# Another order for the opening of an FNet mixing and GeGLU kernel, with the −2·O weights made on GpSimd

## Chip, core and metric

The kernel runs on one core of a Trainium2 chip. The metric is the device time of one execution in microseconds (us). Its engines are called here TensorE (PE in the profile; PEld is its weight load), VectorE (DVE), ScalarE (ACT), GpSimd (POOL) and SyncE (SP, which only issues transfers here).

## What is computed

```python
def _attn_ref(x):                      # x: 8 x 3008 x 256, float32
    X = np.fft.fft(x, axis=1)
    X = np.fft.fft(X, axis=2)
    return X.real.astype(np.float32)

def _moe_ref(x, w_gate, w_val, w_out): # 24064 x 256, 256 x 1536 twice, 1536 x 256
    g = x @ w_gate
    gelu = 0.5 * g * (1.0 + erf(g * np.float32(1.0 / np.sqrt(2.0))))
    val = x @ w_val
    return (gelu * val @ w_out).astype(np.float32)
```

The second is applied to the rows of the first.

## The kernel before, in words

**The mixing.** The DFT over the 3008 tokens is split as 64 times 47. A batch entry is loaded twice, forward and mirrored (a row-indexed transfer on POOL, L163). Folds (`fold_ops`, L221, L222, L225, and for later entries L229) add and subtract the two into `eo`, in five pieces of positions: (13,4), (9,4), (5,4), (1,4) and (0,1), written as (first position, how many). Matmuls with a table `G` follow (`s1`, L508, in four groups of two halves for the first entry; `s1t`, L549, for the others), then for the first entry a combination through identity matrices (`ch`, L530) into `Z`, then matmuls with a table `TP` (`tp_e`, L585 and L590) into two halves `E` and `O`, and a helper row `EB` (`tp_y`, L609). The DFT over the 256 channels is folded into the gate and value weights: `make_w` (L448) multiplies the raw weights by a table `CW`, and its results are evacuated from PSUM into `W_sb` by ACT (L454) or DVE (L456). All tables are computed in the kernel: phases on DVE (`reduced`, L265, L266), sines on ACT (L351 to L374, L408).

**The feed-forward part.** A row t of the spectrum and the row T−t share `E` and `O`: one is E+O and the other E−O. For each of the 12 slices of 128 hidden columns, a gate matmul on E and one on O (L668) give the first row's gate, ACT takes its GELU (L684), and a third matmul with the weights −2·O (called `M`; `l1_gate2`) turns the same PSUM bank into the mirrored row's gate, for a second GELU (L693). In the first chunk's slices 0 to 7 the value does the same with an `M` of its own (`three`, `V3_TO` = 1024 columns; L707 and L724 are the products on DVE). In all other slices the mirrored value is made on DVE (L712, L730) and the product on POOL (L732). L757 multiplies the products by the output weights `Wo_sb`.

**What sets the order.** Every engine executes in the order in which the code emits (`manual_schedule`). `opening()` emits the tables, loads, folds and matmuls of the first entry. `feed()` then emits numbered steps, one for each slice of each chunk (12 steps a chunk, 3 chunks an entry). Step i emits, in this order: gate E and O of slice i; gate M of slice i−1; value of slice i; POOL work from `plan()`; value M or O of slice i−1; and the `fill` of that step from `plan()`. The fills of steps 0 to 7 are the remaining `make_w`: columns 256 to 511 in step 0, 512 to 1023 in steps 1 to 3, 1024 to 1535 in steps 4 to 7. From step 4 on `plan()` gives POOL the folds of the second entry.

**POOL's queue in the opening.** POOL issues 21 transfers in this order: numbers 1 to 5 bring the first entry's rows that are not in `x_stage` (SP brings that one); 6 to 13 are the raw weights, gate and value by turns in column ranges of 256, 256, 512 and 512 (L428); 14 to 19 bring the second entry (L185, L163); 20 and 21 are the two halves of the output weights (`load_wo`, L434). The raw weights and the entries 1 to 5 and 14 to 19 are converted to bf16 on the way.

**The M weights.** `make_w` with part 1 makes O; `minus()` inside it makes M by scaling the PSUM bank with a column `keep2` (−2, and 0 in row 0), on ACT (L463) or on DVE (L465). For columns 0 to 255 the call is held back to the end of the opening.

**Filler matmuls.** `warm(n)` (L828) issues n matmuls of zeros, whose result nobody reads.

Of the kernel before, what the change touches and what calls it, by code (L numbers as in the profile page):

```python
# [10 lines left out]
BF16 = mybir.dt.bfloat16  # L11
AF = mybir.ActivationFunctionType
ALU = mybir.AluOpType
# [15 lines left out]
def kernel(  # L29
# [212 lines left out]
    row_j = const_pool.tile([128, NJ], FP32)  # L242
    row_k = const_pool.tile([128, NK], FP32)
    row_c = const_pool.tile([128, 128], FP32, name="row_c")
    par = const_pool.tile([1, 5, 128], FP32)
    one = const_pool.tile([1, 2], FP32)
    parc = const_pool.tile([128, 5], FP32)
# [16 lines left out]
    def reduced(d, r, f):  # L264
        nc.vector.tensor_scalar(r, f, MAGIC, None, op0=ALU.add)  # L265
        nc.vector.scalar_tensor_tensor(d, r, MAGIC, f, op0=ALU.subtract, op1=ALU.subtract)  # L266
# [14 lines left out]
    def pool_consts2():  # L281
        nc.gpsimd.iota(row_c, pattern=[[1, 128]], base=0, channel_multiplier=0, **IOTA)
        nc.gpsimd.iota(par[:, 0, :], pattern=[[1, 16], [0, 8]], base=1, channel_multiplier=0, **IOTA)
        nc.gpsimd.iota(row_t, pattern=[[1, K1]], base=0, channel_multiplier=0, **IOTA)

    def par_n1():

# [76 lines left out]

    def cw_phases():
        nc.scalar.activation(cf[:, 0:128], row_c, AF.Copy, scale=col_n0)
        reduced(cd[:, 0:128], cr[:, 0:128], cf[:, 0:128])

    def cw_magnitude():
        nc.scalar.activation(cf[:, 128:256], cd[:, 0:128], AF.Abs)  # L370
# [5 lines left out]
    def cw_rest():  # L376


        nc.vector.tensor_copy(CW[:, 0, 0, 0:1], col_e)
        nc.vector.tensor_copy(CW[:, 1, 0, 0:1], col_h)  # L380
        for i, sign in enumerate((1.0, -1.0)):
            nc.vector.tensor_scalar(
                _sub(CW, [[256, 2], [2, 64]], 128 + i), _sub(CW, [[256, 2], [2, 64]], i), sign, None, op0=ALU.mult)
        nc.vector.tensor_copy(CW[:, 1, 1, 0:1], col_h)

    def identities():
# [2 lines left out]
            _sub(II, [[128, 3], [1, 128]], 0), _sub(row_c, [[0, 3], [1, 128]], 0), col_p, None, op0=ALU.is_equal)  # L389
        nc.vector.tensor_scalar(II[:, 1, 1, :], row_c, col_p, -1.0, op0=ALU.is_equal, op1=ALU.mult)  # L390

    def t_columns():
        ps = psum("v")
        for i in range(5):
            nc.tensor.matmul(ps[:, i : i + 1], par[:, i, :], one[:, int(i == 0) : int(i == 0) + 1], start=True, stop=True)
        nc.scalar.activation(parc, ps[:, 0:5], AF.Copy)

    def t_phases():
        k1 = _sub(row_t, [[1, K1]], 0)
        for i in range(2):  # L400
            nc.scalar.activation(
                tf[:, i * K1 : (i + 1) * K1], k1, AF.Identity, scale=parc[:, 0:1], bias=parc[:, 1 + i : 2 + i])

    def t_reduced():
        reduced(td[:, :], tr[:, :], tf[:, :])
# [33 lines left out]

    V3_TO = 1024  # L440

    def make_w(i, f0, n, parts=(0, 1), engine="A", m_at=None, tag="dft"):

        def run():
            ps = psum(tag)
            for k, part in enumerate(parts):
                for half in range(2):
                    nc.tensor.matmul(  # L448
                        ps[:, k * n : (k + 1) * n], CW[:, part, half, :], w_raw[:, i, half, f0 : f0 + n],
                        start=half == 0, stop=half == 1)  # L450
            m = n * len(parts)
            dst = _sub(W_sb, [[F, len(parts)], [1, n]], (2 * i + parts[0]) * F + f0)
            if engine == "A":
                nc.scalar.activation(dst, ps[:, :m], AF.Copy)  # L454
            else:
                nc.vector.tensor_copy(dst, ps[:, :m])  # L456
            if 1 in parts and (i == 0 or f0 < V3_TO):
                def minus():
                    if i and f0 == 0:
                        W["v", "M"] = work([128, V3_TO], BF16, "osb", 3, "w_minus")[:, :]  # L460
                    dst, src = W["gv"[i], "M"][:, f0 : f0 + n], ps[:, m - n : m]
                    if engine == "A":
                        nc.scalar.activation(dst, src, AF.Copy, scale=keep2)  # L463
                    else:
                        nc.vector.tensor_scalar(dst, src, keep2, None, op0=ALU.mult)  # L465

                if m_at is None:
                    minus()
                else:
                    m_at.append(minus)  # L470
        return run
# [44 lines left out]
                nc.vector.tensor_copy(dst, src)  # L516
        return run

    def ch(b, pp, engine="A"):

        def run():
            st = state(b)
            A = st["A"]
            if "Z" not in st:
                st["Z"] = Z_tile()
            ps = ps_any(b)
            for q in range(2):
                k = 2 * (2 * pp + q)
                for g in range(2):
                    nc.tensor.matmul(  # L530
                        ps[:, q * C : (q + 1) * C], _sub(A, [[1, 128]], g * NK * K1 + k * K1), II[:, g, :, :],
                        start=g == 0, stop=g == 1)
            dst = _sub(st["Z"], [[1, 512]], pp * 512)
            if engine == "A":
                nc.scalar.activation(dst, ps[:, :], AF.Copy)
            else:
                nc.vector.tensor_copy(dst, ps[:, :])
        return run

    def s1t(b, jg, half):  # L540
# [252 lines left out]
    def opening():  # L793
        stage[0] = stage_tile()
        xb[0] = xb_tile(0)
        for j0, nj, at in ((9, 8, 0), (0, 1, 8)):
            nc.sync.dma_start(
                out=_sub(stage[0], [[1, nj * C]], at * C),
                in_=ap_replace(x, ap=[[32 * C, NPX], [1, nj * C]], offset=x.offset + j0 * C))
        pool_consts()  # L800
        index_consts(0)
        cast_mirror(0, 9, 8)
        pool_consts2()
        cast_mirror(0, 5, 4)
        cast_forward(0, 1, 8)
        index_consts(1)
        cast_mirror(0, 0, 1)
        cast_mirror(0, 1, 4)
        for f0, n in ((0, 256), (256, 256), (512, 512), (1024, 512)):
            load_w(f0, n)  # L810
        xb[1] = xb_tile(1)
        cast_forward(1, 9, 8)
        cast_mirror(1, 9, 8)
        cast_forward(1, 0, 9)
        for j0, nj in ((5, 4), (1, 4), (0, 1)):
            cast_mirror(1, j0, nj)
        for q in range(2):
            load_wo(q)
        idle = gelu_tile()[:, 0, :]
        nc.vector.memset(one[:, 0:1], 1.0)  # L820
        sin_table()
        nc.vector.memset(idle, 0.0)

        def warm(n):

            ps = psum("o")
            for _ in range(n):
                nc.tensor.matmul(ps[:, :], idle[:, 0:128], idle[:, :], start=True, stop=True)  # L828

        def fold_piece(j0, nj):  # L830
            for f in fold_ops(0, j0, nj, nc.vector):
                f()

        vec_consts()
        vec_fills()
        warm(7)
        g_phases()
        t_columns()
        t_phases()
        g_rows(9, 7)  # L840
        t_reduced()
        vec_consts2()
        identities()
        cw_phases()
        g_ends()
        cw_magnitude()
        vec_fills2()
        g_rows(1, 8)
        t_sin()
        cw_sin()  # L850
        gelu_table()
        warm(6)
        fold_piece(9, 4)
        s1(0, 2, 0)()
        s1(0, 2, 1)()
        warm(8)
        fold_piece(13, 4)
        cw_rest()
        fold_piece(5, 4)
        s1(0, 1, 0)()  # L860
        s1(0, 1, 1)()
        warm(2)
        fold_piece(0, 1)
        s1(0, 3, 0)()
        s1(0, 3, 1)()
        fold_piece(1, 4)
        t_write()
        s1(0, 0, 0)()
        s1(0, 0, 1, "V")()
        minus = []  # L870
        make_w(0, 0, 256, m_at=minus, tag="o")()
        ch(0, 0)()
        ch(0, 1, "V")()
        make_w(1, 0, 256, m_at=minus, tag="g")()
        tp_e(0, 0, 0, "V", tag="v")()
        tp_e(0, 0, 1, "A", tag="v")()
        minus[0]()
        minus[1]()

    def behind_first_gate():  # L880
        tp_y(0, 0)()

    NS = NG * NFC

    def plan():
# [8 lines left out]
            e = "A" if gi == 1 else "V"  # L894
            early += [ch(0, 2 * gi), ch(0, 2 * gi + 1, e), tp_e(0, gi), tp_o(0, gi, e), tp_y(0, gi)]
        for s, f in (
                (0, make_w(0, 256, 256)), (0, make_w(1, 256, 256, engine="V")), 
                (1, make_w(1, 512, 512, (1,))), (2, make_w(0, 512, 512, (0,), "V")), 
                (3, make_w(0, 512, 512, (1,))), (3, make_w(1, 512, 512, (0,), "V")),
                (4, make_w(1, 1024, 512, (1,), "V")), (5, make_w(0, 1024, 512, (0,), "V")),   # L900
                (6, make_w(0, 1024, 512, (1,))), (6, make_yw()), (7, make_w(1, 1024, 512, (0,), "V"))):
            at(fill, s, f)
        for i, f in enumerate(early):
# [56 lines left out]
    def feed():  # L960
# [11 lines left out]
        for i, (parts, fc) in enumerate(blocks):  # L972
# [2 lines left out]
                pend = list(works[i // NFC - 1])  # L975
            two = sooner.pop(i, []) if i <= NFC + 2 else [pend.pop(0) for _ in range(2) if pend]
            parts["G"][fc]()
            if i == 0:
                behind_first_gate()
            if before:  # L980
                before[0]["g"][before[1]]()
            parts["V"][fc]()
# [49 lines left out]
```

## Time and profile before

| what | us |
|---|---|
| median of 8 runs (622.64 to 624.59) | 623.57 |
| the profiled execution's own time | 623.46 |
| its span, first to last instruction | 621.4 |
| TensorE busy | 609.8 (98%) |
| VectorE busy | 576.7 (93%) |
| GpSimd busy | 504.5 (81%) |
| ScalarE busy | 426.3 (69%) |
| first matmul of the feed-forward part starts at | 19.00 |

The profile is of one execution. Times in it count from the span's start; the execution's own time is 2.06 us longer than the span. A row of its timeline has a start, a length, the engine, the source line, the operation, output <- input, and how many instructions were merged; in brackets stands the engine's idle time before the row and what ended it. A row of its stages has the stretch of time, then each engine's busy time (with the number of instructions), the granted TensorE clock (1.00 is full speed), the share of the 16 DMA engines that was busy, and GB/s.

### The profile page before, as it was taken

The page shows a single profiled execution, that of the slowest core. Times are in us where ns is not written, and L with a number is a line of the kernel's source. Part 1 is how long each engine was busy: PE and PEld are TensorE (multiplying, and loading weights), DVE is VectorE, ACT ScalarE, POOL GpSimd, SP SyncE. Part 2 cuts the span into 40 slices and gives each one's busy share as a digit, 9 for nine tenths or more (in the row PEclk, how much of TensorE's full clock was granted, in tenths as well). Part 3 has the DMA queues.
Part 4 walks back from the last instruction along what each step waited for, and adds up shares of the span by engine and source line. Part 5 has one row for each costly group of instructions (what it writes and reads, how often), then busy time and mean ns, then how long its engine had stood idle before and what let it go on. Part 6 is the DMA issues. An engine that isn't in the chain of part 4 may idle for free.

```text
span 621.4 us, 12788 instructions
## 1 busy us (share of the span) xinstructions
PE 609.8 (98%) x4229; PEld 405.7 (65%) x4229; DVE 576.7 (93%) x939; ACT 426.3 (69%) x827; POOL 504.5 (81%) x510
## 2 busy tenths in 40 slices
PE   7999999999999999999999999999999999999997
PEld 3456666666666666666666666666666666666666
DVE  8688998999999999999999999999999999999992
ACT  6877667767776677667766677767676667666661
POOL 8399899999997999879997899969987555555651
PEclk8999999999999999999999999999999999999999
DMA  9961736555463353631644335543122321221123
GB/s 180 232 94 27 202 99 155 119 138 150 114 152 94 103 139 90 177 107 43 168 122 120 103 87 133 136 108 93 48 65 70 95 68 47 65 52 41 42 52 82
DMA packets 52464, 65.40 MB, mean 105 GB/s; under 512 B 7627, under 2 KB 47276, under 8 KB 50002
## 3 DMA queue, kind: packets, MB, share of 16 engines
q1 hardware_dynamic: 45470, 49.03, 30.4%
q0 software_dynamic: 6608, 15.29, 11.6%
q8 instruction: 33, 0.54, 0.4%
q10 hardware_dynamic: 320, 0.26, 0.2%
q14 instruction: 33, 0.27, 0.2%
HBM read 39.65 MB, written 30.17 MB: 112 GB/s over the span
## 4 chain that ended last, share of the span: by engine, by line
PE 90%; POOL 4%; issue 2%; DVE 2%; ACT 1%; DMA 1%; SPq 0%; ACTq 0%; POOLq 0%; DVEq 0%
PE ps_o L757 37%; PE ps_g L668 28%; PE ps_v L668 19%; PE ps_dft L549 2%; POOL h_sb L732 2%; PE ps_dft L585 1%; PE ps_o L828 1%; DMA out_dram<-out_sb 1%; POOL eo_sb L229 1%; POOL ab_sb L222 1%; PE ps_dft L448 0%; POOL ab_sb L225 0%; ACT gelu_sb L693 0%; DVE h_sb L724 0%; ACT gelu_sb L684 0%
## 5 line engine op out<-in xcount | busy, mean ns | idle before, releaser
L732 POOL TENSOR_TENSOR h_sb<-gelu_sb,v_sb 128x512 bf16<-128x512 bf16 (+1 forms) x280 | 319.4, 1145 | 88.4 <-DVE v_sb L730 83.0
L757 PE MATMUL ps_o<-Wo_sb,h_sb 128*128 128x256 bf16 (+1 forms) x2232 | 334.7, 273 | 0.8 <-POOL h_sb L732 0.8
L757 PEld LDWEIGHTS <-h_sb 128*128 128x128 bf16 (+1 forms) x2304 | 228.7, 100 | 112.2 <-POOL h_sb L732 2.4
L684 ACT ACTIVATE gelu_sb<-ps_g 128x512 bf16<-128x512 f32 (+1 forms) x288 | 169.6, 589 | 99.8 <-PE ps_g L668 90.0
L712 DVE SCALAR_TENSOR_TENSOR ve_sb<-EB_sb,yw,ps_v 128x512 f32<-128x512 bf16 (+1 forms) x280 | 206.3, 737 | 22.8 <-PE ps_v L668 18.8
L668 PEld LDWEIGHTS <-W_sb 128*128 128x128 bf16 x1440 | 138.0, 98 | 81.5 <-issue 4.1
L728 DVE TENSOR_TENSOR h_sb<-gelu_sb,ps_v 128x512 bf16<-128x512 bf16 (+1 forms) x280 | 189.7, 677 | 1.1 <-ACT gelu_sb L693 0.7
L730 DVE SCALAR_TENSOR_TENSOR v_sb<-ve_sb,ps_v 128x512 f32<-128x512 f32 (+1 forms) x280 | 187.3, 669 | 0.0
L668 PE MATMUL ps_g<-O_sb,W_sb 128*128 128x512 bf16 (+1 forms) x576 | 168.9, 374 | 0.4 <-DMA O_sb<-yrow 0.3
L693 ACT ACTIVATE gelu_sb<-ps_g 128x512 bf16<-128x512 f32 (+1 forms) x288 | 169.1, 587 | 0.0
L668 PE MATMUL ps_g<-E_sb,W_sb 128*128 128x512 bf16 (+1 forms) x288 | 108.0, 375 | 0.8 <-ACT gelu_sb L693 0.5
L668 PE MATMUL ps_v<-E_sb,W_sb 128*128 128x512 bf16 (+1 forms) x288 | 108.0, 375 | 0.6 <-DVE W_sb L456 0.4
L668 PE MATMUL ps_v<-O_sb,W_sb 128*128 128x512 bf16 (+1 forms) x288 | 108.0, 375 | 0.0
L777 ACT ACTIVATE out_sb<-ps_o 128x512 f32<-128x512 f32 x92 | 54.9, 597 | 35.3 <-PE ps_o L757 35.1
L229 POOL TENSOR_TENSOR eo_sb<-ab_sb 94x512 bf16<-94x512 f32 (+1 forms) x70 | 77.7, 1112 | 0.4
L552 ACT ACTIVATE S_sb<-ps_dft 96x512 bf16<-96x512 f32 x56 | 33.0, 589 | 18.8 <-PE ps_dft L549 18.8
L225 POOL TENSOR_TENSOR ab_sb<-x_raw,x_raw 94x508 f32<-94x508 f32 (+1 forms) x30 | 33.0, 1099 | 0.0
L222 POOL TENSOR_TENSOR ab_sb<-x_raw,x_raw 94x508 f32<-94x508 f32 (+1 forms) x30 | 33.0, 1099 | 0.0
L549 PE MATMUL ps_dft<-eo_sb,G 94*96 94x256 bf16 x119 | 22.3, 272 | 0.5 <-POOL eo_sb L229 0.5
L595 ACT ACTIVATE E_sb<-ps_dft 128x512 bf16<-128x512 f32 (+1 forms) x23 | 13.5, 588 | 8.7 <-PE ps_dft L585 8.7
L163 POOL DMA_INDIRECT x_raw<-in_x_dram,idx x18 | 17.0, 946 | 2.9 <-issue 1.4
L595 ACT ACTIVATE O_sb<-ps_dft 128x512 bf16<-128x512 f32 (+1 forms) x22 | 12.9, 589 | 7.3 <-PE ps_dft L585 6.7
(151 smaller groups left out, 203.7 us busy)
## 6 DMA issues: line engine op xcount, KB each, us to landing
out_dram<-out_sb SPq DMA_DIRECT2D x364, 64.0 KB
x_raw<-in_x_dram SPq DMA_DIRECT2D x10, 768.0 KB
Z_sb<-z SPq DMA_DIRECT2D x7, 768.0 KB
z<-S_sb SPq DMA_DIRECT2D x7, 576.0 KB
EB_sb<-yrow SPq DMA_DIRECT2D x6, 376.2 KB
z<-S_sb SPq DMA_DIRECT2D x7, 192.0 KB
x_raw<-in_x_dram SPq DMA_DIRECT2D x2, 640.0 KB
x_stage<-in_x_dram SPq DMA_DIRECT2D x1, 768.0 KB
```

Source lines behind the costliest of these rows:

```text
L222: eng.tensor_tensor(ab(0, 1, up), fwd(1, up), mir(255, down), op=ALU.add)
L229: eng.tensor_tensor(_sub(eo, [[C, nj], [1, 128]], j0 * C + g * 128), ab(0, 0, [[1, 128]]), ab(1, 0, [[1, 128]]), op=op)
L549: nc.tensor.matmul(ps[:96, q * C : (q + 1) * C], G[:, j, :], _sub(eo, [[1, C]], j * C), start=(j == js[0]), stop=(j == js[-1]))
L668: nc.tensor.matmul(ps[:, :n], W[nm, part][:, fs], src, start=start, stop=stop, **kw)
L684: nc.scalar.activation(gl[:, 0, :n], pg[:, :n], AF.Gelu)
L693: nc.scalar.activation(_sub(gl, [[-1, n]], TOK + n - 1), pg[:, :n], AF.Gelu)
L712: nc.vector.scalar_tensor_tensor(ve[:, :n], EB_bufs[b][:, c0 : c0 + n], yw[:, fc : fc + 1], pv[:, :n], op0=ALU.mult, op1=ALU.add)
L728: nc.vector.tensor_tensor(st["h"][:, fc, 0, :n], gl[:, 0, :n], pv[:, :n], op=ALU.mult)
L730: nc.vector.scalar_tensor_tensor(_sub(vv, [[-1, n]], n - 1), ve[:, :n], 2.0, pv[:, :n], op0=ALU.mult, op1=ALU.subtract)
L732: nc.gpsimd.tensor_tensor(st["h"][:, fc, 1, :n], gl[:, 1, :n], vv[:, :n], op=ALU.mult)
L757: nc.tensor.matmul(pso[:m, half], st["h"][:, fc, sign, h0 : h0 + m], Wo_sb[:, fc, :], start=(fc == 0 and not (first and sign)), stop=(fc = ...
L777: nc.scalar.activation(_sub(osb, [[1, 2 * C]], 0, part_num=m), pso[:m, :], AF.Copy)
```

## The change

- The order of the opening: `t_columns` puts one filler matmul behind each of its five column matmuls and no longer ends with the evacuation, which moves into `t_phases`, and that goes behind the first sines. `identities` and `vec_fills2` go ahead of the folds. The fold of piece (9,4) goes ahead of the range reductions of the CW phases (split off as `cw_reduced`) and of the TP phases (`t_reduced`); the evacuation of its first matmul group goes ahead of the later sines on ACT. A group of two filler matmuls is dropped.
- `cw_rest` makes the sign-changed half of CW with one product by a row of signs (`row_s`, a new `iota` on POOL) in place of two.
- `ch` can do half of its columns; the first two calls become four, whose evacuations go to ACT and DVE by turns. `t_write` moves from ahead of the last `s1` group to behind the first of these. The first two `tp_e` change engines.
- `tp_y(0, 0)` moves from behind the first gate matmuls (step 0) to the fill of step 5.
- `minus()` can go to an engine of its own. In step 0 (both), step 1 (value, columns 512 to 1023) and step 3 (gate, columns 512 to 1023) it goes to POOL, where it scales the finished O weights in SBUF by `keep2`; for the first value columns it goes to DVE.
- The second half of the output weights is issued in the fill of step 2, and no longer in the opening.

```diff
@@ pool_consts2
+        nc.gpsimd.iota(row_s, pattern=[[0, 64], [-2, 2]], base=1, channel_multiplier=0, **IOTA)
@@ cw_rest
-        for i, sign in enumerate((1.0, -1.0)):
-            nc.vector.tensor_scalar(
-                _sub(CW, [[256, 2], [2, 64]], 128 + i), _sub(CW, [[256, 2], [2, 64]], i), sign, None, op0=ALU.mult)
+        nc.vector.tensor_tensor(
+            _sub(CW, [[256, 2], [1, 128]], 128), _sub(CW, [[256, 2], [1, 128]], 0), _sub(row_s, [[0, 2], [1, 128]], 0),
+            op=ALU.mult)
@@ t_columns
             nc.tensor.matmul(ps[:, i : i + 1], par[:, i, :], one[:, int(i == 0) : int(i == 0) + 1], start=True, stop=True)
+            between(1)
@@ make_w, minus
-                    if engine == "A":
+                    if m_engine == "P":
+                        nc.gpsimd.tensor_scalar(dst, W["gv"[i], "O"][:, f0 : f0 + n], keep2, None, op0=ALU.mult)
+                    elif (m_engine or engine) == "A":
@@ opening
-        for q in range(2):
-            load_wo(q)
+        load_wo(0)
...
         g_phases()
-        t_columns()
-        t_phases()
+        columns = t_columns(warm)
         g_rows(9, 7)
-        t_reduced()
         vec_consts2()
         identities()
+        vec_fills2()
         cw_phases()
         g_ends()
+        t_phases(columns)
+        g_rows(1, 8)
+        warm(6)
+        first, second = fold_ops(0, 9, 4, nc.vector)
+        first()
+        s1(0, 2, 0)()
+        second()
+        cw_reduced()
+        t_reduced()
         cw_magnitude()
-        vec_fills2()
-        g_rows(1, 8)
+        cw_sin()
         t_sin()
-        cw_sin()
         gelu_table()
-        warm(6)
-        fold_piece(9, 4)
-        s1(0, 2, 0)()
         s1(0, 2, 1)()
         warm(8)
...
-        warm(2)
         fold_piece(0, 1)
...
         fold_piece(1, 4)
-        t_write()
         s1(0, 0, 0)()
         s1(0, 0, 1, "V")()
         minus = []
         make_w(0, 0, 256, m_at=minus, tag="o")()
-        ch(0, 0)()
-        ch(0, 1, "V")()
-        make_w(1, 0, 256, m_at=minus, tag="g")()
-        tp_e(0, 0, 0, "V", tag="v")()
-        tp_e(0, 0, 1, "A", tag="v")()
+        ch(0, 0, qs=(0,))()
+        t_write()
+        ch(0, 0, "V", qs=(1,))()
+        ch(0, 1, qs=(0,))()
+        ch(0, 1, "V", qs=(1,))()
+        make_w(1, 0, 256, m_at=minus, m_engine="V", tag="g")()
+        tp_e(0, 0, 0, "A", tag="v")()
+        tp_e(0, 0, 1, "V", tag="v")()
@@ plan
-                (0, make_w(0, 256, 256)), (0, make_w(1, 256, 256, engine="V")), 
-                (1, make_w(1, 512, 512, (1,))), (2, make_w(0, 512, 512, (0,), "V")), 
-                (3, make_w(0, 512, 512, (1,))), (3, make_w(1, 512, 512, (0,), "V")),
-                (4, make_w(1, 1024, 512, (1,), "V")), (5, make_w(0, 1024, 512, (0,), "V")), 
+                (0, make_w(0, 256, 256, m_engine="P")), (0, make_w(1, 256, 256, engine="V", m_engine="P")),
+                (1, make_w(1, 512, 512, (1,), m_engine="P")), (2, make_w(0, 512, 512, (0,), "V")),
+                (2, lambda: load_wo(1)), (3, make_w(0, 512, 512, (1,), m_engine="P")), (3, make_w(1, 512, 512, (0,), "V")),
+                (4, make_w(1, 1024, 512, (1,), "V")), (5, make_w(0, 1024, 512, (0,), "V")), (5, tp_y(0, 0)),
@@ feed
-            if i == 0:
-                behind_first_gate()
```

## The prediction

> **What bounds the kernel now.** I read the busy time by stages first, then the timeline around each place where TensorE stops, then the waits of POOL.
>
> ```profile
> 40.00:60.00 20.00, 18.73 (x136) 11.99 (x135) 17.55 (x29) 15.59 (x30) 19.92 (x21) 1.00 0.06 14
> 60.00:100.00 40.00, 39.70 (x283) 26.85 (x282) 37.36 (x59) 27.45 (x55) 38.07 (x40) 1.00 0.58 154
> 100.00:200.00 100.00, 99.84 (x698) 67.80 (x697) 95.41 (x147) 72.02 (x139) 93.22 (x94) 1.00 0.51 130
> ```
>
> The first busy figure is TensorE, the fifth POOL. From 60 us on TensorE is never short of work: a microsecond lost or won there ends in the result one for one. From 40 to 60 it idles 20 − 18.73 = 1.27 us, and POOL is the full engine (19.92 of 20).
>
> ```profile
> 27.03 0.88 POOL L434 DMA_DIRECT2D Wo_sb<-in_moe_w_out_dram  x1 [4.60 <-DMA w_raw<-in_moe_w_gate_dram]
> 29.31 0.85 POOL L434 DMA_DIRECT2D Wo_sb<-in_moe_w_out_dram  x1 [1.40 <-DMA w_raw<-in_moe_w_val_dram]
> 32.19 0.21 POOL L221 TENSOR_TENSOR ab_sb<-xb 94x8 f32<-94x8 bf16 x1 [2.03 <-DMA xb<-in_x_dram,idx]
> 56.14 2.52 POOL L229 TENSOR_TENSOR eo_sb<-ab_sb 94x512 bf16<-94x512 f32 x2
> 58.72 0.38 PE L549 MATMUL ps_dft<-eo_sb,G 94*96 94x256 bf16 x2 [0.45 <-POOL eo_sb L229]
> ```
>
> These are rows of the timeline. POOL begins the second entry's folds at 32.19, when their rows have landed, works without a gap, and at 58.66 releases a TensorE that waited for it. So the stretch from 32.19 to 58.7 hangs on a landing, not on the opening: **an opening that is shorter by any amount still meets 58.7.**
>
> The first two rows matter more. POOL stood still for 4.60 us before it could issue the first half of the output weights (transfer 20 of its queue), until the gate weights of columns 1024 to 1535 (transfer 12) were in, and again at transfer 21 for transfer 13. At transfer 19 the waits show the same pattern (2.2 us for transfer 11). A transfer of POOL waits for the eighth before it, and whatever is behind it in POOL's queue waits too. Before the change nothing urgent is behind it.
>
> **The opening, priced at nothing.** DVE runs without a gap from 7.02 to 14.5. What the change takes from ahead of the first fold are the TP reductions (0.23 + 0.29) and the CW reductions (0.22 + 0.29). `identities` (0.60 + 0.28) waits for nothing but `row_c`, so it follows `g_phases` (end 5.85), and DVE is free for the fold at about 7.1 and not 8.61. The rows must be there: POOL's queue had moved the 0.39 MB of the mirrored part at about 7.2 (0.14 MB to 6.0, 0.21 MB in the next us); with a landing at 7.6 the gain is 1.0 us. But the 1.03 us of reductions then lie between this fold and the next, so fold (1,4) ends near 13.9, as before (13.86). ACT has the evacuation of the first group (0.46) more ahead of the GELU table load, which ends near 12.8 for 12.17.
>
> `cw_rest` now waits for sines on ACT that end near 11.1 to 11.4; behind it in DVE's queue are folds (5,4), (0,1) and (1,4), and it comes up at 11.4, so I price that wait at nothing (at most 0.3). Its product of 256 columns in place of two of 128 (0.38 together) lies between 0.2 and 0.42 (the 508-column fold in bf16); no difference. `row_s` on POOL costs 0.26 (`row_c`, same size) ahead of transfer 2; the DMA engines are full at that time (share over 1.0), so nothing.
>
> Behind fold (1,4) there is a gain. The two fillers at 13.39 (1.05 us) are gone. The last ACT evacuation of `s1` ends near 15.2 (16.04 before). `ch` in four halves evacuates on two engines at once (about 0.45 for each of 256 columns, after L463's 0.47) where before 0.60 and 0.69 followed each other. `t_write` (0.74) leaves the way of the last `s1` evacuation and runs while ACT clears its own. Without `tp_y`, the first value matmul follows the gate at once. First gate pair near 18.1, for 19.00 and 19.44: **1.3 us earlier**; value 1.5 us.
>
> The next `make_w` needs value columns 512 to 1023 (12.22 issued, landed 9.0 us later, 21.2): step 1 meets that wait (0.3 to 0.5 us). All this ends at the stall below, which a transfer sets, so its worth is 0; without that stall it ends at POOL's 58.7, and is worth 0 too.
>
> **The M weights on POOL: the stall.** In `feed`, the gate M of slice 2 (third matmul of step 3) reads columns 256 to 383 of M. The `minus()` of these columns now sits in POOL's queue behind `load_wo(0)`.
>
> ```profile
> 25.52 0.59 PE L668 MATMUL ps_g<-O_sb,W_sb 128*128 128x512 bf16 x2
> 3.04 0.26 POOL L282 IOTA row_c<- 128x128 f32 x1
> 61.90 0.45 POOL L229 TENSOR_TENSOR eo_sb<-ab_sb 94x128 bf16<-94x128 f32 x1
> 34.69 2.49 POOL L229 TENSOR_TENSOR eo_sb<-ab_sb 94x512 bf16<-94x512 f32 x2
> ```
>
> The first row holds that matmul, the second of two 0.21 apart: it starts at 25.73. After the change it can't start before 27.03 + 0.88 (issue) + the `minus()` of 256 columns. No row shows a one-input scaling on POOL. A 128-column generator takes 0.26 and a product of two inputs 0.45 (128 columns) or 1.24 (512); so 256 columns lie between 0.3 and 1.24. I take 0.55, nearer to the 128-column rows. With 0.06 for the hand-over (58.66 to 58.72), 28.5. That is **2.8 us later** than 25.73 (2.5 to 3.5).
>
> Behind it wait, on TensorE, everything; on POOL the other `minus()`: value 256 (0.55, done at 29.0; wanted 0.65 after the gate M, at 29.2), value 512 (about 1, to 30), transfer 21 (0.85, to 30.9) and gate 512 (its O is evacuated near 30.5; done at 31.9, wanted in step 5, after 32). The folds start at 32.19 as before. If a scaling costs as much as the two-input row, they start 0.5 later, which TensorE, late by then, doesn't meet. ACT loses 0.50 + 0.68 + 0.68 and DVE 0.47, which are hidden: in the stall both are idle.
>
> The Trainium skill, "GPSIMD Engine Reference", section 3.1, gives one-input work about 1.03 cycles an element at 1.2 GHz, an estimate of 0.22 us for 256 columns plus dispatch; by it the stall would be some 0.3 us shorter. No row here shows such an operation.
>
> **tp_y.** Its four matmuls (0.22, from the pitch of rows 19.66 and 19.88) leave step 0, where the stall swallows the gain, and come to step 5, behind the stall: **+0.2**. Its ACT evacuation (0.61) falls where ACT idled 0.93. `EB` is first read in step 8.
>
> **The clock.** TensorE would come to the stall at about 24.0 and stand for 4.4 us.
>
> ```profile
> 5.57 1.47 PE L828 MATMUL ps_o<-gelu_sb 128*128 128x512 bf16 x6
> 9.43 0.34 PE L508 MATMUL ps_g<-G,eo_sb 94*128 94x96 bf16 x4 [2.39 <-DVE eo_sb L222]
> ```
>
> The stages behind it (the granted clock stands before the last two figures):
>
> ```profile
> 11.00:12.00 1.00, 1.00 (x5) 0.37 (x3) 0.97 (x8) 0.99 (x2) 1.00 (x2) 0.55 1.24 187
> 12.00:13.00 1.00, 1.00 (x7) 0.42 (x6) 1.00 (x5) 0.91 (x3) 1.00 (x3) 0.50 1.30 154
> 13.00:14.00 1.00, 1.00 (x10) 0.69 (x8) 1.00 (x6) 0.69 (x2) 1.00 (x3) 0.50 1.28 157
> 14.00:15.00 1.00, 1.00 (x17) 0.76 (x15) 0.52 (x2) 0.40 (x2) 1.00 (x2) 0.74 1.28 165
> ```
>
> A gap of 2.39 us was followed by a clock of 0.50 from about 11.1 to 14.5: 3.4 us at half speed. A gap of 4.4 us should cost the same: 3.4 us of work done at half, 1.7 us lost if it is dense. Step 4 has some 0.5 us of its own idling, so I take **+1.4** (0 if the clock holds, 1.7 at most). The fillers added in the opening prevent the first drop, not this one.
>
> The Trainium skill, "TensorE: Matmul & The Clock Gate", "What's actually happening", lets the clock fall only after an idle window of about 3.4 us. Here a gap of 2.39 was enough; by the rule as by the row the stall drops it, and the sum is the same.
>
> **What is given back.** TensorE's idle time of 40 to 60, where it waited for POOL, goes when TensorE itself is late: **−1.27**. POOL's products of slices 9 to 11 then wait for TensorE's values instead, which costs nothing more.
>
> **Sum.** 2.8 + 0.2 + 1.4 − 1.27 = **+3.1 us**. The profiled execution took 623.46 (span 621.4 and 2.06 around it); that gives 626.6. The median of the runs is 0.11 above this execution, so either base gives 626.6 or 626.7. I predict 626.6.
>
> **Rivals.**
>
> 1. *The stall comes, the clock holds.* 2.8 + 0.2 − 1.27 = +1.7: 625.2. For it: before, TensorE idled 0.45 and 0.60 in these steps at 1.00. Against: the only gap of this length in the trace was followed by a drop.
> 2. *POOL's scaling is dear.* At twice the two-input rate (256 columns: 1.3; 512: 2.5) the `minus()` of the gate's columns 512 to 1023 ends after 27.91 + 1.3 + 1.3 + 2.5 + 0.85 + 2.5 = 36.4 and the folds start then, 4.2 us late; step 5 stalls too. About +4.5: 628. Nothing in the trace speaks for such a rate.
> 3. *No stall*: POOL isn't held by transfer 20, or transfer 12 lands 2 us sooner. Then the gain of 1.3 runs into POOL's fixed 58.7: 623.5, no change. Against: the load order is the same and the DMA engines are full from 2 to 37 us.
> 4. *Faster.* The opening's 1.3 to 1.5 us carry to the end: 622.0. One thing would do it: the second entry's rows land, and POOL begins the folds, that much before 32.19, and `load_wo(0)` with them. It decides from 58.7 minus the shift. Against: as many bytes go before them as now.
>
> **How the numbers follow.** About 0.2% (1.25 us) is what a measurement of this kernel can tell from no change. Forecast 0.50 (slower); rival 1 0.24 (0.18 slower, 0.06 within); rival 2 0.08 (slower); rival 3 0.11 (within); rival 4 0.07 (faster). Together: faster 0.07, within 0.17, slower 0.76. The range leaves out rival 4 and most of rival 2: it goes from 623.4 (rival 3, a tenth below no change) to 628.2 (the sum with a scaling of 1.24, a clock loss of 1.7 and half a microsecond of the give-back missing).
>
> **What would show it.** Right: in the profile after, POOL's first scaling starts directly behind L434 at about 27.9; a gate matmul L668 shows idle time of 4 to 4.5 us, ended by POOL; the clock is near 0.5 for 3 us behind it; step 4 begins at 30 to 32 (27.46 before); TensorE doesn't wait for POOL at L549 near 60. First gate matmul near 18. Wrong: L434 at 24 or sooner, or folds that start well before 32. If the clock stays at 1.00 over the stall, rival 1 holds.

## The result, and the profile after

The changed kernel takes 626.0 us (median of 11 runs, 625.18 to 629.36); the kernel before took 623.95 beside it (32 runs). The ratio is **1.0045 [1.0034, 1.0056]**: slower by 2.1 to 3.5 us. The profiled execution took 626.47 (span 624.7), which is 3.0 us more than that of before. The forecast was 626.6.

The runs fall in two groups that the median hides. Of 13 executions (these 11, the profiled one and one more), nine took 625.2 to 626.5 with a mean granted clock of 0.999 or 1.0, and four took 628.6 to 629.4, all with 0.991. The profile is of the first group. Its lines are numbered 6 to 9 higher: L440 is `load_wo`, L469 POOL's `minus()`, L516 `s1`, L558 `s1t`, L677 the gate and value matmuls, L836 the fillers.

POOL in the timeline of after, to be held against the L434 and L221 rows of before:

```profile
21.98 0.88 POOL L440 DMA_DIRECT2D Wo_sb<-in_moe_w_out_dram  x1 [0.24 <-issue]
25.34 0.93 POOL L469 TENSOR_SCALAR W_sb<-W_sb,keep 128x256 bf16<-128x256 bf16 x1 [2.48 <-ACT W_sb L460]
...
31.17 0.90 POOL L440 DMA_DIRECT2D Wo_sb<-in_moe_w_out_dram  x1 [2.12 <-DMA w_raw<-in_moe_w_val_dram]
32.11 1.57 POOL L469 TENSOR_SCALAR W_sb<-W_sb,keep 128x512 bf16<-128x512 bf16 x1
34.63 0.21 POOL L221 TENSOR_TENSOR ab_sb<-xb 94x8 f32<-94x8 bf16 x1 [0.95 <-DMA xb<-in_x_dram,idx]
...
58.59 2.50 POOL L229 TENSOR_TENSOR eo_sb<-ab_sb 94x512 bf16<-94x512 f32 x2
```

`load_wo(0)` is issued at 21.98 and waits for no transfer (27.03 after 4.60 of waiting before). **The stall that the forecast is built on is not in this execution**: the first scaling waits for ACT, which writes the O weights, and TensorE waits only 0.32 for a scaling. The folds start 2.44 later than before (32.19), on a landing again, and the products at L229 that release `s1t` come 2.45 later.

TensorE in the same timeline:

```profile
8.99 0.61 PE L836 MATMUL ps_o<-gelu_sb 128*128 128x512 bf16 x1
...
10.04 3.38 PE L836 MATMUL ps_o<-gelu_sb 128*128 128x512 bf16 x7
13.22 0.52 PE L516 MATMUL ps_g<-G,eo_sb 94*128 94x96 bf16 x4
...
21.75 0.38 PE L677 MATMUL ps_g<-E_sb,W_sb 128*128 128x512 bf16 x1 [0.32 <-issue]
23.36 0.38 PE L677 MATMUL ps_g<-O_sb,W_sb 128*128 128x512 bf16 x1 [1.23 <-DVE O_sb L606]
...
61.15 0.38 PE L558 MATMUL ps_dft<-eo_sb,G 94*96 94x256 bf16 x2 [0.23 <-POOL eo_sb L229]
```

The first gate matmuls start at 21.75 and 23.36 (19.00 and 19.44 before), so the opening is 2.75 and 3.9 us later, where the forecast had 1.3 earlier. Step 8 starts at 39.64 (35.83 before): 3.8 late.

The stages of after, with columns as in the prediction:

```profile
40.00:60.00 20.00, 19.55 (x145) 12.53 (x143) 18.65 (x31) 16.20 (x32) 19.84 (x20) 1.00 0.07 17
60.00:100.00 40.00, 39.46 (x280) 26.64 (x278) 36.41 (x58) 28.15 (x55) 37.93 (x40) 1.00 0.53 138
```

TensorE's idle time between 40 and 60 shrinks from 1.27 to 0.45, which gives 0.8 back; from 60 to 100 it is 0.54 for 0.30. So 3.8 − 0.8 + 0.2 = 3.2, against a span that is 3.3 longer. That this number is so near the forecast is luck: it came by another way.

**Where the opening lost its time.** The next rows of after are of POOL, VectorE (twice) and SP:

```profile
3.70 0.83 POOL L286 IOTA row_s<- 128x128 bf16 x1
3.26 1.30 DVE L340 TENSOR_SCALAR ff<-ff 94x24 f32<-94x24 f32 x1
14.94 0.16 DVE L383 CAST CW<-col 128x1 bf16<-128x1 f32 x1 [1.88 <-ACT CW L377]
17.90 1.27 SPq L157 DMA_DIRECT2D x_raw<-in_x_dram  x3
```

- `row_s` took 0.83 and not the 0.26 of the forecast. POOL's second transfer went out at 4.70 (3.88 before), the fifteenth at 16.28 (15.32 before). While POOL made it, the small product at L340 took 1.30 on VectorE (0.34 before), and all that VectorE does next is a microsecond later.
- In TensorE's queue the fillers ran at half rate: 7 of them in 3.38 us, 0.43 apart, where later matmuls of 512 columns are 0.21 apart. VectorE had the first half of the fold ready at 9.96 (L222 there: 9.28 + 0.68); the first `s1` matmul started at 13.22, behind the last filler. The column for the clock reads 1.00 here, so this slow rate shows in the pitch alone.
- ACT evacuates that group ahead of the last sines, and so these came late; `cw_rest` waited 1.88 for them, with the last folds behind it.
- The last fold frees the buffer into which SP loads the third entry's forward rows (`x_raw`, 1.67 MB). SP issued them at 17.90, 4 us later than before:

```profile
13.89 1.74 SPq L157 DMA_DIRECT2D x_raw<-in_x_dram  x3
```

This last row (of before) leads to the theory. `x_raw` goes through SP's queue and competes with POOL's for the DMA engines. Before, it came at 13.89, and transfer 12 landed at 27. After, it came at 17.90, and transfer 12 was in by 21.98.

### The profile page after: what moved, and what is told of

Its sections match the earlier page's. It is cut to its first block, busy times and chain, and to the rows that moved or that the text cites. A ratio compares the mean times of both kernels' runs of the same rounds, so it can differ in the third digit from the quotient of the medians.

```text
span 624.7 us, 12794 instructions
## 1 busy us (share of the span) xinstructions
PE 613.5 (98%) x4232; PEld 407.4 (65%) x4232; DVE 577.8 (92%) x939; ACT 424.6 (68%) x824; POOL 510.9 (82%) x515
## 4 chain that ended last, share of the span: by engine, by line
PE 86%; POOL 7%; DMA 3%; issue 2%; SPq 1%; DVE 0%; ACT 0%; POOLq 0%; DVEq 0%; ACTq 0%
PE ps_o L766 37%; PE ps_g L677 27%; PE ps_v L677 18%; DMA w_raw<-in_moe_w_val_dram 3%; PE ps_dft L558 2%; POOL eo_sb L229 2%; PE ps_dft L594 1%; POOL h_sb L741 1%; POOL ab_sb L222 1%; DMA out_dram<-out_sb 1%; POOL w_raw L434 1%; POOL ab_sb L225 1%; POOL xb L163 1%; SPq L671 1%; DVE v_sb L739 0%
## 5 line engine op out<-in xcount | busy, mean ns | idle before, releaser
L677 PEld LDWEIGHTS <-W_sb 128*128 128x128 bf16 x1440 | 138.1, 98 | 82.6 <-issue 4.6
L677 PE MATMUL ps_g<-O_sb,W_sb 128*128 128x512 bf16 (+1 forms) x576 | 169.1, 375 | 1.9 <-DVE O_sb L606 1.2
L677 PE MATMUL ps_v<-E_sb,W_sb 128*128 128x512 bf16 (+1 forms) x288 | 108.0, 375 | 0.6 <-DVE W_sb L462 0.4
L677 PE MATMUL ps_g<-E_sb,W_sb 128*128 128x512 bf16 (+1 forms) x288 | 108.0, 375 | 0.3 <-issue 0.3
L677 PE MATMUL ps_v<-O_sb,W_sb 128*128 128x512 bf16 (+1 forms) x288 | 108.0, 375 | 0.0
L229 POOL TENSOR_TENSOR eo_sb<-ab_sb 94x512 bf16<-94x512 f32 (+1 forms) x70 | 77.6, 1111 | 0.5
L222 POOL TENSOR_TENSOR ab_sb<-x_raw,x_raw 94x508 f32<-94x508 f32 (+1 forms) x30 | 32.9, 1096 | 0.0
L558 PE MATMUL ps_dft<-eo_sb,G 94*96 94x256 bf16 x119 | 22.3, 272 | 0.2 <-POOL eo_sb L229 0.2
```

The source lines that it names most:

```text
L222: eng.tensor_tensor(ab(0, 1, up), fwd(1, up), mir(255, down), op=ALU.add)
L229: eng.tensor_tensor(_sub(eo, [[C, nj], [1, 128]], j0 * C + g * 128), ab(0, 0, [[1, 128]]), ab(1, 0, [[1, 128]]), op=op)
L677: nc.tensor.matmul(ps[:, :n], W[nm, part][:, fs], src, start=start, stop=stop, **kw)
```

## The experiments

**Theory**: what decides is a race on the DMA engines. If `x_raw` is issued early, POOL's queue all but stops beside it (in before it moved 0.03 MB from 21 to 22 us), `load_wo(0)` waits, and with POOL's `minus()` behind it TensorE stalls. If the opening is late, `x_raw` is late too and there is no stall; the lateness is paid instead. **Rival**: the opening's own costs (`row_s`, fillers) make the time, and the transfers follow. A second rival is POOL's slow scaling alone.

Medians of the kernel before, run beside each set of these, were 623.69 to 623.82.

| kernel | median us (runs) | ratio to before |
|---|---|---|
| e1: before + POOL's M part | 624.76 (10) | 1.0022 [1.0007, 1.0037] |
| e2: after without POOL's M part | 625.82 (7) | 1.0026 [1.0014, 1.0037] |
| e3: after without fillers between columns | 629.21 (4) | 1.0090 [1.0072, 1.0108] |
| e4: before, late `x_raw` | 621.25 (4) | 0.9957 [0.9940, 0.9973] |
| e5: after, late `x_raw` | 623.95 (11) | 0.9999 [0.9986, 1.0011] |
| e6: e3, late `x_raw` | 621.58 (10) | 0.9970 [0.9961, 0.9980] |
| e7: after without `row_s` | 625.44 (10) | 1.0028 [1.0012, 1.0044] |
| e8: before, late `x_raw`, tail of the opening | 621.53 (10) | 0.9967 [0.9958, 0.9976] |
| e9: before + unused `row_s` | 625.03 (11) | 1.0018 [1.0009, 1.0027] |
| e10: before + fillers between columns | 624.19 (11) | 1.0009 [1.0000, 1.0018] |
| e11: e1, late `x_raw` | 621.30 (5) | 0.9959 [0.9946, 0.9972] |
| e12: e6 without `row_s` | 621.71 (10) | 0.9969 [0.9959, 0.9980] |

### The two halves of the change

e1 takes the `m_engine="P"` lines and the moved `load_wo(1)` into before; e2 takes them out of after (`minus()` on ACT and DVE, both `load_wo` in the opening).

> The kernel before, with only the POOL part of the change: four minus() on POOL and the second half of the output weights in step 2 (tp_y stays in step 0, the opening is as before). Forecast's reason (stall): the first entry's folds end at 13.9 as before, so the third entry's rows are issued then, transfer 12 lands near 27 and load_wo(0) is issued at 27.0; the first scaling starts at 27.9 and takes 0.93 (measured in the changed kernel), the gate M of slice 2 starts near 28.9 (25.73 before), the folds start near 33.8, and the time is 1.6 to 3.2 us over before: 625.5 to 627.2. Rival (all of the loss is in the opening): load_wo(0) is issued near 22, the scalings are hidden, folds at 32.2, 624.0.

> The changed kernel with its opening (row_s, fillers between the columns, halves of ch, tp_y in step 5), but the M weights on ACT and DVE and both halves of the output weights in the opening, as before. Theory landing (the end follows the start of POOL's second-entry folds, and that the landing of transfer 15): transfer 15 is issued near 16.3 and lands near 34.5 as in the changed kernel, first gate matmul near 21.8, folds at 34.6 for 32.2, time 2.4 over before: 626.4, no different from the changed kernel. Rival (the loss is POOL's scalings, and the late opening costs nothing): 624.0.

Either half alone is slower, and neither profile holds a stall of the forecast size. e1's 624.76 lies below the 625.5 to 627.2 of its theory and above its rival's 624.0; e2 came at 625.82, with folds at 34.53 as expected but a first gate at 19.69 and not 21.8. In e1's profile the columns and fillers of the opening ran at half rate, `x_raw` went out at 15.32, and `load_wo(0)` waited only 1.28 (timeline of e1):

```profile
21.87 0.88 POOL L434 DMA_DIRECT2D Wo_sb<-in_moe_w_out_dram  x1 [1.28 <-DMA w_raw<-in_moe_w_gate_dram]
```

This execution took 623.67. Five of the ten took 625.3 to 627.2, with clocks of 0.992 to 0.998, and five 623.2 to 624.2, so the median stands between two groups; none of the slower five was profiled. In e2 the fillers between the columns ran at full rate (a pair 0.63 after the other, 1.06 in after), `x_raw` went out at 15.85, and POOL waited (timeline of e2):

```profile
28.08 0.88 POOL L440 DMA_DIRECT2D Wo_sb<-in_moe_w_out_dram  x1 [6.04 <-DMA w_raw<-in_moe_w_gate_dram]
...
31.38 0.60 PE L454 MATMUL ps_dft<-w_raw,CW 128*128 128x512 bf16 x2 [1.47 <-DMA w_raw<-in_moe_w_val_dram]
...
34.53 0.22 POOL L221 TENSOR_TENSOR ab_sb<-xb 94x8 f32<-94x8 bf16 x1 [2.06 <-DMA xb<-in_x_dram,idx]
```

Here the wait for transfer 12 is 6.04, but no `minus()` is behind it. TensorE stands 1.47 all the same, because its own `make_w` waits for the late value weights of transfer 13. The folds are as late as in after without any scaling ahead of them, so POOL's scalings are not what delays them there.

### The stall made visible

The edit of e3:

```diff
-        columns = t_columns(warm)
+        columns = t_columns(lambda n: None)
```

> The changed kernel without the five filler matmuls between the column matmuls, nothing else. Theory fillers (the first folded group waits in TensorE's queue behind fillers that run at half rate): the first s1 matmul moves from 13.2 to about 10 to 11, fold (1,4) ends near 15, the first gate matmul comes near 19. The third entry's rows are then issued near 15 instead of 17.9, and transfer 12 lands later than in the changed kernel, so load_wo(0) waits again: by the forecast's reason it is issued at 25 to 27 and the gate M of slice 2 waits for POOL 1 to 3 us. Time within 1 us of the changed kernel, 625 to 627. Rival (the opening alone sets the end): 3 us less than the changed kernel, 623.0.

e3 takes five fillers away, its opening is 2.5 us sooner (first gate 19.25), and it is **slower** than after by 3.2 us, beyond the 625 to 627 expected. `x_raw` went out at 15.54. The timeline of e3, and then its stages:

```profile
29.40 0.88 POOL L440 DMA_DIRECT2D Wo_sb<-in_moe_w_out_dram  x1 [7.38 <-DMA w_raw<-in_moe_w_gate_dram]
30.32 0.95 POOL L469 TENSOR_SCALAR W_sb<-W_sb,keep 128x256 bf16<-128x256 bf16 x1
31.32 0.61 PE L677 MATMUL ps_g<-O_sb,W_sb 128*128 128x512 bf16 x1 [5.95 <-POOL W_sb L469]
```

```profile
25.00:30.00 5.00, 0.38 (x2) 0.00 (x0) 1.23 (x3) 0.60 (x1) 0.60 (x1) 0.80 1.08 220
30.00:35.00 5.00, 3.68 (x10) 1.28 (x11) 1.33 (x3) 1.19 (x2) 4.72 (x6) 0.52 1.06 208
```

This is the chain of the forecast: POOL waits for transfer 12, the scaling starts directly behind the issue, and the gate M waits for it, idle for 5.95. Between 25 and 30 TensorE is busy for 0.38 us; in the next 5 us the granted clock is 0.52.

### The opposing transfer moved

In e4 (and in every "late" kernel) `x_raw` is issued from ACT's queue in steps 8 and 9 instead of from SP in the opening. This is called late rows below; it changes the queue along with the moment, and no run parts the two. The edit, shortened at `...`:

```diff
-def load_forward(b, j0, nj):
+def load_forward(b, j0, nj, queue=None):
...
-            nc.sync.dma_start(
+            (queue or nc.sync).dma_start(
...
-  at(fill, s, lambda k=k: load_part(2, k, (load_forward,)))
+  at(fill, s, lambda k=k: load_forward(2, *((9, 8), (1, 8), (0, 1))[k], nc.scalar))
```

> The kernel before, with one edit: the third entry's forward rows (1.67 MB) are issued from ACT's queue in steps 8 and 9 (near 36 us) and not from SP as soon as their buffer is free (13.9). Theory landing: the raw weights and the second entry's rows share the DMA engines with less, transfer 12 lands near 21 to 22 and transfer 15 at 26 to 29 instead of 32.0, POOL starts the folds 3 to 6 us sooner and TensorE's idle time between 40 and 60 (1.27 us) goes: 1.0 to 1.5 us under before, 622.5 to 623.0. Rival (the end follows the first gate matmul, which stays at 19.0): no change, 624.0.

e4 is 2.5 us faster than before, more than the 1.0 to 1.5 expected. The queues between 15 and 30 us show why; the columns are packets, MB and share. First before:

```profile
q0 software_dynamic: 1261, 1.78, 68.0%
q1 hardware_dynamic: 336, 1.67, 42.7%
```

Then e4, where the second queue has no line:

```profile
q0 software_dynamic: 2306, 2.96, 115.0%
```

POOL's queue (q0) moves 2.96 MB where it moved 1.78 beside the 1.67 MB of `x_raw`: it lost 1.18 MB to that load. `load_wo(0)` goes out at 20.71 without a wait, the folds start 6.3 us sooner, and TensorE doesn't run dry behind them. The timeline and the stages of e4:

```profile
25.88 0.21 POOL L221 TENSOR_TENSOR ab_sb<-xb 94x8 f32<-94x8 bf16 x1 [2.84 <-DMA xb<-in_x_dram,idx]
```

```profile
40.00:50.00 10.00, 9.90 (x73) 6.27 (x71) 9.72 (x17) 8.15 (x16) 6.06 (x7) 1.00 0.61 157
50.00:60.00 10.00, 10.00 (x79) 6.94 (x77) 9.33 (x15) 8.20 (x17) 10.00 (x11) 1.00 0.14 34
```

TensorE idles 0.10 there, for 1.27 before.

> The changed kernel with the third entry's forward rows issued from ACT's queue in steps 8 and 9. Theory race (POOL's scalings are harmless or stall TensorE for 4 to 6 us according to whether these rows overtake transfer 12 on the DMA engines; the folds start with transfer 15): transfer 12 lands near 21 to 22 always, no wait of TensorE for POOL before 35, folds start near 28 or sooner; then the opening sets the end, and that depends on whether the fillers run at half rate: 621.5 with a first gate pair near 19.7, up to 625 with one near 23. No run near 629. Rival (POOL's scalings cost by their own length, 4.97 us, whatever the transfers do): the folds are late all the same and the time stays near 626.

> The kernel without fillers between the columns (629.2), with the late rows as well. Theory race: the stall of 5.95 us before the gate M of slice 2 and the drop of the clock behind it are gone, first gate pair at 19.3 and 19.7 as there: 621 to 621.7, that is 7.5 to 8 us less from the order of one load. Rival (the stall is the length of POOL's queue itself): the stall shrinks by less than half, over 625.

e6 is the decisive one: the same edit on e3 gives **7.6 us** (629.21 to 621.58), with folds at 29.17 and no stall, because `load_wo(0)` waits 0.39 where it waited 7.38 (timeline of e6):

```profile
22.45 0.88 POOL L440 DMA_DIRECT2D Wo_sb<-in_moe_w_out_dram  x1 [0.39 <-DMA w_raw<-in_moe_w_gate_dram]
```

On after (e5) it gives 2.05 us, and the group near 629 is gone. e5 has two groups of its own: four runs at 622.3 to 623.3 (clock 0.995 or 0.996), seven at 623.9 to 624.6 (0.998 or more). The profiled one is of the latter: half-rate fillers between the columns, first gate at 21.59, folds at 31.28 (near 28 expected). So late rows cure the stall and not the late opening.

e5 and e6 differ by the five fillers alone: 623.95 and 621.58, first gate at 21.59 and 18.96. With the race out of the way, the fillers between the columns cost 2.4 us for a first gate 2.6 us later, which prices the late opening by itself.

### `row_s`

e7 takes the `iota` of `row_s` away and makes the sign change by two products, as before; e9 adds the `iota` alone to before, used by nobody.

> The changed kernel without row_s: cw_rest makes the sign-changed half with two scalings, as before. Theory: the 0.83 us of the bf16 generator on POOL goes, the next transfer is issued 0.8 us sooner (3.9 for 4.70), the DVE scaling that took 1.30 us beside it takes 0.34 again, and all of the opening moves up 0.8 to 1.0 us. By theory race the third entry's rows then come sooner too, so that transfer 12 is overtaken more often: time between 625 and 629, not better. Rival (the opening's length sets the end): 1 us less than the changed kernel, 625.

> The kernel before with one instruction more: POOL generates row_s (128x128 in bf16) behind row_t; nobody reads it. Theory landing: 0.83 us on POOL, the DVE scaling of 94x24 beside it takes 1.30 for 0.34 us, transfers 2 to 21 are issued 0.8 to 0.9 us later, the second entry's folds start at 33.0 to 34.0 for 32.2, and the time is 0.8 to 1.5 us over before, though TensorE's own work is the same: 624.6 to 625.3. Rival (the end hangs on the opening's matmuls, which wait for the first rows of x and not for these transfers): no change, 623.8.

The unused `row_s` costs 1.3 us (623.69 to 625.03). In e9 it takes 0.83, L340 takes 1.29 (0.34 to 0.36 in the kernels without it, e7 and e10), transfer 2 goes out at 4.70, the first gate starts at 19.87 (0.87 late) and the folds at 32.70 (0.5 late).

The Trainium skill, "Advanced Engine Details and Errata", "Mode Summary", says that VectorE's second SBUF port is shared with GpSimd, and that GpSimd's instructions and those of VectorE that use both ports block each other. The rows of L340 agree with such a block; that L340 uses both ports, or that the port is the cause, no run here shows.

The profiled execution of e7 has full-rate fillers between the columns, a first gate at 18.59, and this timeline:

```profile
26.60 0.88 POOL L438 DMA_DIRECT2D Wo_sb<-in_moe_w_out_dram  x1 [5.92 <-DMA w_raw<-in_moe_w_gate_dram]
27.51 0.95 POOL L467 TENSOR_SCALAR W_sb<-W_sb,keep 128x256 bf16<-128x256 bf16 x1
28.51 0.61 PE L675 MATMUL ps_g<-O_sb,W_sb 128*128 128x512 bf16 x1 [3.80 <-POOL W_sb L467]
```

It took 626.3. Scaling at 27.51 (27.9 forecast), gate M at 28.51 (28.5), 626.3 (626.6): the forecast's picture, in a kernel that differs from after by `row_s`. Its runs took 623.8 to 624.8 (five, clock 0.997 to 1.0) or 626.1 to 628.2 (five, 0.991 to 0.995), so e7 goes both ways too.

### Fillers, and the tail of the opening

e10 puts the fillers between the column matmuls into before. e8 takes from the change, on e4, the halves of `ch`, the later `t_write`, the dropped fillers, the changed `tp_e` engines and `tp_y` in step 5.

> The kernel before with one filler matmul behind each of the five column matmuls, nothing else. Theory fillers: the runs part in two groups. Where TensorE is already at full rate when they begin (a pair every 0.63 us) the columns end near 8, the tables on ACT that wait for them move 2 us, and the time is 624 to 625; where it is at half rate (a pair every 1.06 us) they end near 10, the first gate pair comes 3 to 4 us later, at 22 to 23, and the time is 626 to 627. Rival (fillers are free, since TensorE idles there): one group at 623.8.

> The kernel before with the late rows, and of the change only the last part of the opening: ch in halves on two engines, t_write behind the first of them, the two fillers dropped, the first two tp_e on the other engines, tp_y in step 5. No row_s, no fillers between the columns, no new fold order, M on ACT and DVE. Theory: with POOL's folds no longer setting the end, the 1.3 us that the forecast worked out for this part come through: first gate pair near 18, time 1.0 to 1.5 us under the kernel before with late rows: 619.8 to 620.3. Rival (the opening's length never reaches the end): 621.3.

Both expectations missed. e10's runs are one group (623.2 to 625.3) and not two. Its profiled execution has half-rate fillers and a first gate at 21.48, 2.5 us late, and still took only 624.16. Its folds start at 31.82, so POOL sets the end near 58 as before, and TensorE's idle time pays for the late opening (stages of e10):

```profile
40.00:60.00 20.00, 19.84 (x147) 13.32 (x149) 19.14 (x31) 16.05 (x32) 19.37 (x20) 1.00 0.06 14
```

Step 8 is still 2.5 us late (38.31 for 35.83); then idle time falls from 1.27 to 0.16, and from 60 to 100 by 0.2. That gives 1.3 back of 2.5, and this execution took 0.7 more than that of before; the last half microsecond I have not located. In e8 the first gate starts at 19.26, as in e4 (19.30), and the time is the same: `ch` waits 0.74 for ACT's evacuation of `s1`, so halves do not help while ACT is the chain.

### Is there a better combination?

> The kernel before with the POOL part of the change and with the third entry's rows issued late: a candidate for the best version. Theory race: transfer 12 lands near 21, no stall; ACT and DVE are spared 2.3 us of scalings in steps 0 to 3, and the 0.45 us that TensorE waited there for a GELU goes: 620.5 to 621.2, against 621.25 for late rows alone. Rival (POOL's 4.97 us of scalings push the folds past the point where TensorE waits): over 622.

> The changed kernel without fillers between the columns, without row_s, and with the late rows: all that the change brought except for what the runs so far showed to cost. Theory: first gate pair 0.8 us sooner than in the same kernel with row_s (19.0 and 19.4), 620.5 to 621.0 for 621.58. Rival (the first rows of x set the opening's start, not POOL's queue): 621.5.

With late rows POOL's M weights neither cost nor gain (e11 621.30, e4 621.25), though the folds start 3.8 us later than in e4 (29.70, directly behind the last scaling, for 25.88). That answers the second rival. Without `row_s` and fillers (e12) the first gate is at 18.19, 0.8 sooner than in e6, and the time is the same within the intervals: 621.71, the rival's number and not the 620.5 to 621.0 of the theory. e4, e6, e8, e11 and e12 can't be told apart; the simplest, e4, is before with one transfer issued later, and beats both kernels.

## Why the prediction came out

The direction, the size and the interval held; the profiled way did not, so that the number agrees is luck. The forecast's own sign of being wrong, L434 at 24 or sooner, came true there (21.98). In that execution the late opening cost what the stall was to cost, and the four executions in which I infer the stall took 628.6 to 629.4, above the 628.2 at which the forecast's range ends. By its steps:

- **What bounds.** Right. A landing sets POOL's folds and these release `s1t`; e4 moved the landing and gained 2.5 us.
- **The opening, "1.3 us earlier".** Wrong by 3.65 us in the profiled run (21.75 for 18.1). Three terms were mis-sized: `row_s` (0.26 taken, 0.83 measured, and 0.96 on L340, which was not in the sum); the wait of `cw_rest` (at most 0.3 taken, 1.88); and the fillers between the columns, to which the sum gave no price and which I took to prevent the first drop of the clock. In an in-order queue ahead of the first `s1` they held TensorE until 13.2. Where they ran at full rate and `row_s` was away (e7, 18.59), the forecast's 18.1 was half a microsecond off; without these fillers and `row_s`, and with late rows (e12, 18.19), it held.
- **The stall, "+2.8".** Right as a mechanism, not as a certainty. "The load order is the same" was the argument against rival 3. It holds for POOL's queue and overlooks SP's: the moment of `x_raw` follows from the last fold. The forecast left that fold at 13.9, so its transfer 12 stayed late; in after the fold ended at 17.88. TensorE stands 3.80 in e7 and 5.95 in e3, and after's profile has no stall. The table below the list sorts the executions.
- **The scaling, 0.55 for 256 columns.** It took 0.91 to 0.95, and 1.56 for 512 (about 1 was taken); the bounds (0.3 to 1.24) held the first. The estimate from the Trainium skill, "GPSIMD Engine Reference", section 3.1, was 0.22 for 256 columns before dispatch; the step from 256 to 512 columns alone took 0.63 here, and the measurement decides.
- **The clock, "+1.4".** A drop comes with the stall in e3 (0.50 from 28, inside the stall, to past 34) and in e7 (0.57 from 28 to 32); after's profile has none. I did not separate its price from the stall's. That a gap of 2.39 caused the first drop is not shown: in e7 the clock is 0.50 from 8 to 10 though TensorE had worked from 4.4 on without a gap, so a gap is not needed (stages of e7):

```profile
8.00:10.00 2.00, 2.00 (x6) 0.66 (x5) 1.78 (x6) 1.71 (x4) 2.00 (x3) 0.50 1.10 214
```

- **The give-back, −1.27.** It was 0.8 in after. The +0.2 of `tp_y` I did not measure by itself.
- **Rival 3** (no stall) had its condition fulfilled in the profiled run, but its 623.5 supposed an opening 1.3 earlier and folds in place. Both came late.

The moment of `x_raw` alone doesn't tell where transfer 12 comes late: e1 issued it at 15.32, between e7 and e3, and has no stall. How long behind transfer 12 it was issued does, in all eight profiles with early rows:

| profile | transfer 12 issued | `x_raw` issued | behind by | `load_wo(0)` waits for transfer 12 |
|---|---|---|---|---|
| before | 12.93 | 13.89 | 0.96 | 4.60 |
| e2 | 14.44 | 15.85 | 1.41 | 6.04 |
| e3 | 13.95 | 15.54 | 1.59 | 7.38 |
| e7 | 12.95 | 14.62 | 1.67 | 5.92 |
| e9 | 13.97 | 15.83 | 1.86 | 5.38 |
| e1 | 12.94 | 15.32 | 2.38 | 1.28 |
| after | 13.93 | 17.90 | 3.97 | none |
| e10 | 12.93 | 17.44 | 4.51 | none |

So the time of the first group is mostly the price of a late opening; the late folds have a smaller share. e5's profiled execution, with folds 3.35 us sooner than after's, has a span 2.3 shorter: 1.8 of that is there at step 8 already (37.83 for 39.64), 1.3 of it from one wait, the evacuation of O by VectorE (22.61 in after, 21.30 in e5). That leaves 0.5 for what comes behind step 8.

For the second group, 628.6 to 629.4 at clock 0.991, I infer the stall: e3 differs from after by fillers alone and took 629.2 with it; with late rows (e5) no run is near 629; and a mean of 0.991 over 627 us stands for some 11 us at half clock (0.009 x 627 / 0.5), where e3's profile has two drops, from about 7.4 to 14.2 and from 28 to 34.4. The clock alone doesn't mark the group, since e3's runs took 628.8 to 630.6 at 0.988 to 0.997. No such execution of after was profiled, so that is argued, not shown.

**Open.** Why VectorE began the evacuation of O only at 22.61 in after, having stood idle for 2.01. What makes the folds of e2 and after land at 34.5, when `row_s` alone gives 32.70 and the fillers alone 31.82. And what decides whether the same matmuls run at full or half rate: before and e1 have the same opening up to there, and the ten column matmuls at 4.4 took 1.24 us in the one and 2.26 in the other.

## What to carry to other kernels

Before a small compute step is put behind a transfer's issue in an engine's queue, look up what that issue waits for, and then which transfers of other queues share the DMA engines and what releases them: a shorter opening released a large load sooner and made the kernel slower. Filler matmuls are work in an in-order queue, and what they delay must be priced at the slow rate. And when a landing bounds, look for a transfer that nobody needs yet and that can be delayed: here that small edit gained the most.

## What the runs showed of the hardware

- A bf16 `iota` of 128x128 on POOL took 0.83 us, the f32 one of the same size 0.26; a VectorE scaling beside it went from 0.34 to 1.30.
- A one-input scaling on POOL in bf16 took 0.93 us for 256 columns and 1.56 for 512, more than the product of two 512-column inputs (1.16).
- With 1.67 MB in SP's queue, POOL's queue moved 1.78 MB in 15 us, and 2.96 without it.
- Behind the first seven fillers some executions had full-rate matmuls, and then 3.4 us or more at a clock of 0.50 that began within 7 us (before, e2, e3, e7); others ran at half rate (512 columns 0.43 apart) to about 10 us or past it while the clock column read 1.00 (after, e1, e10, e12). So a mean clock of 1.0 doesn't mark the better execution: in e5 it goes with the slower group, in e4 with the faster runs (620.8 at 1.0, 621.7 and 622.0 at 0.996 and 0.997).
